# Another order of the pieces in a hand-listed attention and MLP kernel

## The chip, the core and the metric

The kernel runs on one core of a Trainium2 chip. The core has five engines that run their own instruction streams and wait for each other by semaphores: TensorE (PE in the profile; PEld is its weight load), VectorE (DVE), ScalarE (ACT), GpSimd (POOL) and SyncE (SP), which here only issues DMAs. The metric is the device time of one execution in microseconds. Three timed runs of the kernel before gave 219.97, 220.22 and 221.33 us; the median is 220.22.

## The reference

The input x has 2048 rows (tokens) of 512 bfloat16 values. The result is x + A(n) + B(n), where n is x after a layer norm without weights.

```
xn = layernorm(x)                                # rows of 512
A: q, k, v = xn @ wq, xn @ wk, xn @ wv           # 32 heads of 16
   for each of 4 segments of 512 tokens:
     p     = softmax(q k^T / 4 + mask)           # mask: 0 on and below the diagonal, -1e9 above
     a_dot = p v
     a_mem = (phi(q) M) / (phi(q) z + 1e-6)      # phi(t) = t + 1 if t > 0 else exp(t)
     o     = g a_mem + (1 - g) a_dot             # g = sigmoid(beta), one per head
     M, z += phi(k)^T v, sum of phi(k)
   A = o @ wo
B: silu(xn @ w1) @ w2                            # 1792 hidden columns
out = x + A + B
```

## The kernel before

The whole program is a list of some 1350 words, `ORDER`, that is walked once. Each word names a piece, a Python function that issues the few instructions of one step, with its indices: `h0.3.1` is part 1 of hidden tile 3 of segment 0. The word order is the program order of every engine at once: it fixes the order in which each engine runs its own instructions, the order of the DMAs on SP's queue, and the order in which the buffers of each pool are taken (the buffer that was given back first, in the order of the list, is taken first). The engines then run as far ahead of each other as their semaphores let them.

The pieces, with the lines that matter:

- `S0` to `S71` (`scores`): one batch of attention logits, 18 a segment in two groups of nine. TensorE multiplies q and k in four row groups (L724) into `psS`, a tile of four PSUM banks of which there is only one; ScalarE takes the exponential of all 2048 columns (L730, `Pb`); GpSimd zeroes what is above the diagonal (L744). The next batch can be multiplied only when this exponential has been read out of `psS`.
- `k`, `q`, `v`, `h` (`dense`, `dense_mm`): parts of the projections and of the hidden layer, by L336 (whole array) or L338 (four column strips of 32). A part of `k`, `q`, `v`, `h` in segments 0 and 1 is one product's worth of 512 columns, in segments 2 and 3 two. The result of a group of parts stands in one of the four PSUM banks of the pool `pp` until it is taken out.
- Taken out by VectorE: `kv`, `qv`, `vv` (copies, L376, L399, L406), `hv` (L497, with the tanh of `ha`, L492 on ScalarE, before it), `Ev`, `Ov` (L821, L828); by ScalarE: `ka`, `qa`, `va`, `Ea`.
- `E`, `O` (`weigh`, L791): weights times values for even and odd heads; `Om` (L835) merges the odd heads on VectorE.
- `fp`, `fa`, `fv` and `gp`, `ga`, `gv`: phi of k and of q on GpSimd, ScalarE and VectorE (L433); `t` turns phi(k) by a DMA; `m`, `mv`, `mw`: the memory M; `s`, `sv`, `r`, `w`, `R`, `W`, `z`, `zv`, `d`, `dv`, `n`, `nv`: denominators, their spreading by DMAs, and the sums with the memory's part (`zv` L589, `dv` L599, `nv` L608, `R` L560, `W` L566).
- `xs`, `xg`, `Nv`, `XD`: statistics (L286, L289), root (GpSimd) and normalisation (L315) of a tile of 128 tokens, and its transposition by a DMA (L857) for tiles 4 to 15. The first four tiles are transposed on TensorE (`X`, L845).
- `o`, `oc`, `od`, `oh`: full, half and quarter products of the two output projections; `st`, `sh` add x and store. `xl` loads x again. `lw0`, `lw1` load w2 and wo from ScalarE's queue (L169).

Whether a dense product is issued whole or in four strips follows from the words around it (`ahead`, `now`): products next to `E`, `O`, `s` and `m` are issued in strips.

Of the kernel before, what the change touches and what calls it, by code (L numbers as in the profile page):

```python
# [25 lines left out]
S6 fa0.3 k1.2.0 k1.2.1 k1.2.2 h0.5.0 h0.5.1 h0.5.2 q1.1.0 h0.5.3 ha0.5 k1.2.3 kv1.2 q1.1.1 q1.1.2 hv0.5
S8 h0.7.0 q1.1.3 qv1.1 h0.6.0 h0.6.1 h0.6.2 h0.6.3 ha0.6 fv0.3 E1 Ev1 k1.0.0
S9 hv0.6 h0.7.1 h0.7.2 h0.7.3 Om0 ha0.7 k1.0.1 k1.0.2 kp1.2 q1.0.0 q1.0.1 q1.0.2 fp0.1 Nv9 XD9 xs12 k1.0.3 kv1.0 kp1.0
S10 h0.8.0 hv0.7 h0.8.1 h0.8.2 h0.8.3 ha0.8 h0.9.0 h0.9.1 q1.0.3 t0.3 Nv10 XD10 h0.9.2 h0.9.3 qv1.0
S13 hv0.8 O1 Ov1 xs15 v1.0.0 v1.0.1 v1.0.2 ha0.9 v1.0.3 vv1.0 h0.10.0 h0.10.1 bmask  # L30
S12 k1.1.0 k1.1.1 k1.1.2 t0.2 k1.1.3 kv1.1 h0.10.2 h0.10.3 ha0.10 hv0.9 h1.0.0 Om1 h1.0.1 h1.0.2
# [16 lines left out]
S31 o0.0.4 h1.13.0 h1.13.1 h1.13.2 h1.13.3 ha1.13 o0.3.8 Om5 o0.3.11 o0.3.16 hv1.2 o0.3.9
S30 o0.3.14 h1.12.0 h1.12.1 h1.12.2 h1.12.3 t1.3 Nv15 hv1.13 ha1.12 XD15 od0.0.0.0 o0.1.16 od0.1.8.2 o0.1.17 o0.1.12 hv1.12 oc0.1.9.0
S33 o0.0.1 od0.1.8.3 o0.3.1 xl0.1 od0.1.8.0 st0.0 oc0.1.3.0 o0.1.13 oc0.1.3.1 xl0.3 gp1.3 Om4 fa1.0 o0.1.2 E6 o0.1.0  # L50
S32 kp2.3 Ev6 O6 Ov6 o0.3.17 o0.3.13 o0.3.10 o0.1.6 oc0.3.2.1 o0.1.15 m1.2 fa2.0 mv1.2 fv1.0
S35 o0.1.4 q2.2.0 q2.2.1 qv2.2 fp2.0 ga1.3 v2.0.0 v2.0.1
S34 h1.5.0 h1.5.1 o0.1.14 o0.1.11 t1.0 vv2.0 h1.5.2 oc0.3.0.1 xl1.0 gv1.3 fp1.1 h1.5.3 ha1.5 E7
# [889 lines left out]
```

## Time and profile before

| | |
|---|---|
| timed runs, us | 219.97, 220.22, 221.33 (median 220.22) |
| profiled execution, from its first to its last instruction | 218.2 us |
| median less that span | 2.0 us |
| TensorE busy | 210.9 us, 97% of the span, 3982 matmuls recorded |
| weight loads busy | 116.1 us, 4006 instructions |
| VectorE busy | 181.3 us, 83% |
| ScalarE busy | 184.1 us, 84%; of this the 72 exponentials 135.2 us |
| GpSimd busy | 127.4 us, 58% |
| DMA queues | 19.60 MB, 33273 packets |

Columns of the profile's groups: line, engine, operation, output and inputs, shapes, count, then busy time, mean ns of one, and the idle time of the engine ahead of them with what ended it. In a timeline the columns are start, length, engine, line and operation with the count merged into the row. A busy TensorE is not TensorE at its peak: matmuls are pipelined and their recorded ends overlap the next ones.

### The profile page before, as it was taken

The numbers are of one execution on the slowest core, as the hardware profiler recorded it, in microseconds if no ns is written. First come the engines' busy times: TensorE is split into PE (matmuls) and PEld (weight loads), VectorE is DVE, ScalarE is ACT, GpSimd is POOL, SyncE is SP. The second block draws the span as 40 slices with busy tenths as digits, with TensorE's granted clock in tenths as the row PEclk, the third lists the DMA queues.
The fourth block names the chain that finished last, engine by engine and source line by source line (L and its number), as shares of the span: only waits on it lengthen the run. The fifth ranks groups of instructions, "written<-read, shape, count | busy, mean of one in ns | idle before, by whom it ended". The sixth has DMA issues, their size and how long they took to land.

```text
span 218.2 us, 9267 instructions
## 1 busy us (share of the span) xinstructions
PE 210.9 (97%) x3982; PEld 116.1 (53%) x4006; DVE 181.3 (83%) x370; ACT 184.1 (84%) x173; POOL 127.4 (58%) x203
## 2 busy tenths in 40 slices
PE   7899999999999999999999999999999999999994
PEld 7666656655544544455444545445464544465653
DVE  6899999999799899667979886887979897858844
ACT  3799999999999999999999999999989998942000
POOL 6067676789568984697766436962787473410000
PEclk9999999999999999999999999999999999999999
DMA  6996249322200430541125131420042120412223
GB/s 183 344 375 160 51 125 243 74 53 53 51 5 17 157 71 10 117 95 40 49 67 83 54 97 28 74 77 6 0 132 73 52 73 13 131 32 79 84 66 98
DMA packets 33273, 19.60 MB, mean 90 GB/s; under 512 B 14672, under 2 KB 33232, under 8 KB 33232
## 3 DMA queue, kind: packets, MB, share of 16 engines
q1 hardware_dynamic: 30608, 16.39, 28.7%
q10 hardware_dynamic: 2624, 2.62, 3.8%
...
q14 instruction: 10, 0.08, 0.1%
HBM read 9.96 MB, written 2.10 MB: 55 GB/s over the span
## 4 chain that ended last, share of the span: by engine, by line
PE 92%; DMA 3%; ACT 2%; issue 1%; SPq 1%; DVE 0%
PE ps L336 26%; PE psO L338 17%; PE ps L338 16%; PE psS L724 11%; PE psO L336 9%; PE psV L791 8%; PE psS L338 4%; DMA wk_sb<-in_A_wk_dram 3%; ACT Pb L730 2%; PE psM L452 1%; SPq L169 0%; SPq L158 0%; PE ps L509 0%; ACT th L492 0%; DVE o_half L668 0%
## 5 line engine op out<-in xcount | busy, mean ns | idle before, releaser
L730 ACT ACTIVATE Pb<-psS 128x2048 bf16<-128x2048 f32 x72 | 135.2, 1878 | 4.7 <-PE psS L724 2.4
L744 POOL TENSOR_SCALAR_AFFINE_SELECT Pb<-Pb 128x512 bf16<-128x512 bf16 (+2 forms) x88 | 62.3, 718 | 22.4 <-ACT Pb L730 19.6
L497 DVE SCALAR_TENSOR_TENSOR hT<-th,ps 128x512 bf16<-128x512 bf16 x56 | 38.0, 682 | 10.1 <-ACT th L492 9.4
L744 POOL TENSOR_SCALAR_AFFINE_SELECT lows<-Pb 64x512 bf16<-64x512 bf16 (+1 forms) x40 | 24.3, 607 | 32.0 <-ACT Pb L730 24.9
L338 PE MATMUL psO<-w_sb,hT 128*32 128x512 bf16 (+2 forms) x696 | 41.4, 321 | 0.0
L336 PE MATMUL ps<-xnT,w_sb 128*128 128x512 bf16 (+1 forms) x177 | 35.9, 330 | 0.2 <-issue 0.2
L492 ACT ACTIVATE th<-ps 128x512 bf16<-128x512 f32 x56 | 33.0, 594 | 3.5 <-PE ps L338 3.1
L338 PEld LDWEIGHTS <-hT 128*32 128x32 bf16 x864 | 21.5, 96 | 14.6 <-issue 3.1
L338 PE MATMUL ps<-xnT,w_sb 128*32 128x512 bf16 (+1 forms) x408 | 24.8, 349 | 0.0
L724 PE MATMUL psS<-qT,k 32*128 32x64 bf16 (+3 forms) x512 | 23.0, 233 | 0.2
L336 PEld LDWEIGHTS <-w_sb 128*128 128x128 bf16 x178 | 16.4, 98 | 11.9 <-issue 1.2
L336 PE MATMUL psO<-w_sb,hT 128*128 128x512 bf16 (+2 forms) x82 | 20.5, 324 | 0.7 <-issue 0.6
L791 PEld LDWEIGHTS <-Vz 128*32 128x32 bf16 x768 | 16.1, 97 | 9.5 <-issue 0.6
L791 PE MATMUL psV<-Pb,Vz 128*32 128x448 bf16 (+7 forms) x512 | 21.0, 286 | 0.0
L724 PEld LDWEIGHTS <-k 32*128 32x128 bf16 x512 | 9.3, 92 | 21.2 <-issue 20.4
L336 PE MATMUL ps<-xnT,wk_sb 128*128 128x256 bf16 (+1 forms) x63 | 14.4, 326 | 0.4 <-DMA wk_sb<-in_A_wk_dram 0.2
L724 PE MATMUL psS<-qT,kT 16*128 16x448 bf16 (+3 forms) x256 | 14.7, 269 | 0.0
L338 PEld LDWEIGHTS <-w_sb 128*32 128x32 bf16 x408 | 10.3, 96 | 6.7 <-issue 1.7
L621 DVE SCALAR_TENSOR_TENSOR o_out<-psO,x_res 128x512 bf16<-128x512 f32 x14 | 9.4, 679 | 5.0 <-PE psO L338 3.9
L336 PEld LDWEIGHTS <-hT 128*128 128x128 bf16 x92 | 8.5, 98 | 9.6 <-issue 2.1
L828 DVE CAST odd<-psV 128x512 bf16<-128x512 f32 x16 | 11.0, 687 | 2.4 <-PE psV L791 2.4
L338 PE MATMUL psO<-wo_sb,oT 128*32 128x512 bf16 x140 | 12.8, 379 | 0.0
...
## 6 DMA issues: line engine op xcount, KB each, us to landing
...
```

Source lines behind the costliest of these rows:

```text
L336: return [nc.tensor.matmul(out, lhsT=lhsT, rhs=rhs, start=start, stop=stop, skip_group_check=True)]
L338: nc.tensor.matmul(out[c : c + 32], lhsT=lhsT[:, c : c + 32], rhs=rhs, start=start, stop=stop, tile_position=(0, c), skip_group_check=True,)
L452: nc.tensor.matmul(psM[32 * g : 32 * g + 32, i, :].rearrange("p (r d) -> p r d", d=DH), lhsT=st["phiK", dt][:, j, 32 * g : 32 * g + 32], r ...
L492: nc.scalar.activation(out=th[:], in_=sts[s]["h", ft][:, :], func=AF.Tanh, scale=0.5)
L497: nc.vector.scalar_tensor_tensor(out=st["hT"][:, ft, :], in0=st.pop(("th", ft))[:], scalar=1.0, in1=st.pop(("h", ft))[:, :], op0=ALU.add, ...
L621: out = nc.vector.scalar_tensor_tensor(out=o_out[:], in0=st.pop(("psO", j)), scalar=0.5, in1=st["x", j][:], op0=ALU.mult, op1=ALU.add)
L724: nc.tensor.matmul(psS[:, g, c : c + q2 - q1], lhsT=keys[rows], rhs=st["qT"][rows, dt, q1:q2], start=True, stop=True, tile_position=(32 * ...
L730: exp = nc.scalar.activation(out=blocks(Pb, b).rearrange("p y g c -> p g y c"), in_=psS[:, :, :].rearrange("p g (y c) -> p g y c", c=BLOCK ...
L744: over[id(Pb)].append(nc.gpsimd.affine_select(out=out, in_=in_, compare_op=ALU.is_ge, fill=0.0, base=base, pattern=[[0, out.shape[1]], [1, ...
L791: nc.tensor.matmul(psV[32 * g : 32 * g + 32, q0 : q0 + nq].rearrange("p (y c) -> p y c", y=weights.shape[2]), lhsT=Vzs[s % 2][:, kt, 4 * d ...
L828: copy(out=odd[:], in_=sts[s].pop(("psV", 1))[:, :])
```

## The change

Only the list is exchanged. The same 1349 words stand in it; each occurs once in both. Up to `v0.0.0` the two lists agree, and the order of `S0` to `S71` among themselves is the same in both. From there on nearly all other words may stand elsewhere. Some of the moves, cut from the list:

```diff
 ORDER = """
 ones0 ones1 zeros xc0 xd0 ... X1.1 Xa0.1 v0.0.0
-v0.0.1 v0.0.2 xs3 xi2 Nv2 xq3 xi3 v0.0.3 X2.1 Xa1.1 k0.1.0 tb Nv3 X3.1 Xv2.1 k0.1.1 Xv3.1 vv0.0 odd omask k0.0.0 ... xs5 ka0.1 kp0.1
-S0 v0.1.0 v0.1.1 xs6 xs7 q0.2.1 v0.2.1 v0.2.2 v0.2.3 vv0.2 fa0.0 k0.2.0 k0.2.1 k0.2.2 xs4 xg4.4
-S2 q0.2.2 q0.2.3 qv0.2 k0.2.3 kv0.2 fp0.2 fa0.2 v0.1.2 v0.1.3 vv0.1 Nv5 Nv6 XD6 q0.1.0 q0.1.1 q0.1.2 q0.1.3 qv0.1
-S1 h0.0.0 h0.0.1 h0.0.2 xs10 h0.0.3 v0.3.0 v0.3.1 v0.3.2 v0.3.3 ha0.0 vv0.3 q0.3.0 kp0.2 hv0.0
-S3 h0.3.0 h0.3.1 q0.3.1 q0.3.2 h0.3.2 tanh XD5 h0.3.3 k0.3.0 Nv7 XD7 q0.3.3 qv0.3 k0.3.1 xs8 ha0.3
-S4 Nv4 h0.1.0 k0.3.2 h0.1.1 hv0.3 XD4 h0.2.0 h0.2.1 h0.2.2 h0.2.3 ha0.2 xs9 k0.3.3 kv0.3 hv0.2
-S7 xs11 xg8.4 v1.2.0 v1.2.1 v1.2.2 v1.2.3 vv1.2 h0.1.2 h0.1.3 ha0.1 E0
...
-S17 h1.10.3 k1.3.0 hv1.0 k1.3.1 k1.3.2 k1.3.3 kv1.3 fp1.3 h0.12.0 h0.12.1 xs14 m0.2 mv0.2 ha1.10 h0.12.2
+xs3 xq3 xi2 v0.0.1 Nv2 Xa1.1 tb xi3 v0.0.2 Nv3 v0.0.3 X2.1 X3.1 k0.1.0 Xv2.1 k0.0.0 Xv3.1 ... vv0.0 q0.0.3 kf0.0 xs6 xs5 k0.1.2 xl0.0 ... xs4 v0.2.0 kp0.1
+S0 k0.2.0 xs7 v0.2.1 v0.2.2 k0.2.1 q0.2.1 v0.2.3 v0.1.0 fa0.0 v0.1.1 k0.2.2 xg4.4 vv0.2
+S2 q0.2.2 k0.2.3 v0.1.2 v0.1.3 q0.2.3 q0.1.0 q0.1.1 q0.1.2 kv0.2 q0.1.3 qv0.2 fa0.2
+S1 v0.3.0 h0.0.0 qv0.1 Nv4 v0.3.1 v0.3.2 XD4 vv0.1 h0.0.1 Nv6 h0.0.2 h0.0.3 v0.3.3 q0.3.0 fp0.2 Nv5 XD6 ha0.0 vv0.3 xs10 XD5
+S3 h0.3.0 h0.3.1 k0.3.0 h0.3.2 tanh h0.3.3 q0.3.1 ha0.3 k0.3.1 q0.3.2
+S4 k0.3.2 xs8 hv0.0 k0.3.3 q0.3.3 kp0.2 hv0.3 h0.2.0 h0.2.1 h0.2.2 h0.2.3 v1.2.0 kv0.3 ha0.2 lw0 Nv7 v1.2.1 qv0.3
+S7 h0.1.0 xs11 h0.1.1 hv0.2 v1.1.0 v1.2.2 h0.1.2 v1.2.3 vv1.2 h0.1.3 ha0.1 v1.1.1 xs9 xg8.4 E0 hv0.1 fv0.2
+S5 h0.4.0 XD7 h0.4.1 v1.1.2 v1.1.3 h0.4.2 q1.2.0 vv1.1 h0.4.3 Ev0 ha0.4 q1.2.1 q1.2.2 hv0.4
...
+S17 k1.3.0 k1.3.1 k1.3.2 xl0.2 k1.3.3 hv1.0 h1.10.3 ha1.10 XD10 Ov2 kv1.3 h0.12.0 h0.12.1 m0.2 kp1.1 kp1.3
...
```

In the list before, `lw0` stands in the stage of `S11`; in the new one in that of `S4`. `xl0.0`, which stood in that of `S14`, comes ahead of `S0`. `XD13` and `XD15` stood in the stages of `S27` and `S30` and now stand in those of `S35` and `S34`. Behind `S71` the order on VectorE was and is:

```diff
-hv3.13 R0.2 dv3.3 Ov15 R0.1 R0.3 st2.1 dv3.2 R0.0 W0 hv3.10 R1.0 hv3.6 dv3.1 zv3.2 R1.2 R1.3 nv3.2 R1.1 W1 zv3.1 nv3.1 zv3.0 Om15 nv3.0 zv3.3 nv3.3 st2.3 st3.0 st3.2 sh1 st3.1 sh0
+Om14 Om13 hv3.13 R0.3 R0.0 hv3.6 Ov15 R0.2 R0.1 W0 dv3.0 st2.1 dv3.2 R1.1 R1.3 hv3.10 zv3.2 R1.2 R1.0 dv3.1 Om15 W1 nv3.2 zv3.1 nv3.1 dv3.3 st2.3 zv3.0 nv3.0 zv3.3 nv3.3 st3.0 st3.2 sh1 st3.1 sh0
```

More of the change, by code (lines that the diff above doesn't have):

```diff
@@ L26 @@
[L26 to L31, printed above, removed]
@@ L48 @@
[L48 to L53, printed above, removed]
@@ new lines @@
+S11 q1.2.3 fp0.3 fv0.0 v1.3.0 v1.3.1 O0 k1.2.0 v1.3.2 fa0.1 Ov0 k1.2.1
+S6 k1.2.2 qv1.2 kind h0.5.0 h0.5.1 h0.5.2 k1.2.3 t0.2 gate h0.5.3 v1.3.3 q1.1.0 omask kv1.2 q1.1.1 ha0.5
+S8 h0.6.0 vv1.3 q1.1.2 h0.6.1 k1.0.0 q1.1.3 hv0.5 h0.6.2 kp0.3 qv1.1 h0.6.3 E1 Nv8 h0.7.0 fa0.3 Nv10 Ev1 ha0.6
+S9 h0.7.1 h0.7.2 h0.7.3 k1.0.1 k1.0.2 k1.0.3 q1.0.0 hv0.6 t0.0 ha0.7 q1.0.1 q1.0.2 fv0.3 kv1.0
+S10 xs15 h0.9.0 h0.9.1 h0.8.0 XD8 Nv9 h0.9.2 h0.8.1 h0.8.2 hv0.7 q1.0.3 XD9 h0.8.3 ha0.8 h0.9.3
+S13 v1.0.0 v1.0.1 kp1.0 t0.3 qv1.0 v1.0.2 bmask v1.0.3 hv0.8 O1 h0.10.0 h0.10.1 ha0.9
@@ new lines @@
+S12 vv1.0 xs12 k1.1.0 k1.1.1 k1.1.2 hv0.9 h0.10.2 Ov1 h0.10.3 h1.0.0 k1.1.3 h1.0.1 h1.0.2 ha0.10 kv1.1
+S15 E2 h1.10.0 h1.0.3 fp0.1 Nv11 h1.10.1 XD11 hv0.10 Ev2 h1.10.2 Om1 O2 ha1.0
+S17 k1.3.0 k1.3.1 k1.3.2 xl0.2 k1.3.3 hv1.0 h1.10.3 ha1.10 XD10 Ov2 kv1.3 h0.12.0 h0.12.1 m0.2 kp1.1 kp1.3
+S21 q1.3.0 q1.3.1 h0.12.2 xs14 q1.3.2 mv0.2 q1.3.3 h1.3.0 h1.3.1 h0.12.3 ha0.12 qv1.3 h1.3.2
+S14 gp1.2 h1.3.3 hv1.10 h0.13.0 ha1.3 hv0.12 xl0.3 xs13 k2.2.0 fv0.1 k2.2.1 h0.13.1 h0.11.0 h0.13.2
+S16 h0.11.1 h0.11.2 kv2.2 t0.1 hv1.3 fp1.3 Om0 kp1.2 h0.13.3 h0.11.3 q2.1.0 q2.1.1 qv2.1 E3 ha0.13 Ev3 ha0.11
```

108 lines of the change are left out of this document (54 added, 54 removed).

## The prediction

> **What bounds the kernel now.** I read the page first, its busy times and the chain, then the waits of TensorE, then timelines of single stages.
>
> ```profile
> span 218.2 us, 9267 instructions
> ...
> PE 210.9 (97%) x3982; PEld 116.1 (53%) x4006; DVE 181.3 (83%) x370; ACT 184.1 (84%) x173; POOL 127.4 (58%) x203
> ...
> PE 92%; DMA 3%; ACT 2%; issue 1%; SPq 1%; DVE 0%
> ```
>
> TensorE is busy for 97% of the span and is 92% of the chain that ended last. Idle are 218.2 - 210.9 = 7.3 us. The waits say where (first and last of six rows), and one row of the timeline shows the last matmul:
>
> ```profile
> PE psS L864 <- DVE zraw L188: 1.1, 1, 1.1
> ...
> PE ps L336 <- DVE z L468: 0.2, 1, 0.2
> ```
>
> ```profile
> 214.98 0.28 PE L338 MATMUL psS<-wo_sb,oT 128*32 128x256 bf16 x4
> ```
>
> 1.1 us lie ahead of the first matmul and 218.2 - 215.26 = 2.9 us behind the last, for the last evacuation and store; both ends are the same in the two lists. 3.3 us are left for the 214 us between. The only wait there for a piece of VectorE behind the start is 0.2 us. So the old order already feeds TensorE without a break, and a new order can win at most these 3.3 us. No word is added or removed: counted in the lists, both give the same products and 144 changes between whole-array, row-group and strip products, of the same four kinds; the new list issues six weight loads fewer.
>
> There is one more floor, which no wait shows. Here is the stage of `S4`, in which the old list has eight parts (`h0.1.0 k0.3.2 h0.1.1 h0.2.0 h0.2.1 h0.2.2 h0.2.3 k0.3.3`):
>
> ```profile
> 21.55 0.21 PE L724 MATMUL psS<-qT,k 32*128 32x64 bf16 x4
> 21.89 0.39 PE L336 MATMUL ps<-xnT,w_sb 128*128 128x256 bf16 x2
> 22.01 1.88 ACT L730 ACTIVATE Pb<-psS 128x2048 bf16<-128x2048 f32 x1
> 22.34 1.25 PE L336 MATMUL ps<-xnT,w_sb 128*128 128x256 bf16 x10
> 23.93 0.40 PE L724 MATMUL psS<-qT,k 32*128 32x64 bf16 x8
> ```
>
> `S7` starts at 23.93, 0.04 behind the end of the exponential at 22.01 + 1.88 = 23.89, since `psS` is a single tile. From `S4` to `S7` are 2.38 us: a stage can't be shorter, whatever stands in it. Ten matmuls of 256 columns take 1.25, of which the last alone is 0.38 at most, so one is (1.25 - 0.38)/9 = 0.10 to 0.11 and a part of two 0.216. The batch itself is 21.89 - 21.55 = 0.34, and with the change of mode behind the stage about 0.46. A stage of nine parts is 9 x 0.216 + 0.46 = 2.40, just above the floor; one of eight is 2.19 and wastes 0.19.
>
> **The change, part by part.**
>
> *Stages that are too short.* I filled each of the 71 stages of both lists with these prices (a quarter product 0.054, an `E` or `O` 0.54 for its 1280 columns in strips, an `m` 0.13) and added what is missing to 2.38. Old list: 0.19 in `S4`, 0.06 to 0.09 each in `S7`, `S13`, `S17`, `S24` and `S32`, some hundredths in three more: 0.7 us. New list: `S3` has eight parts (0.19), `S17` seven and an `m` (0.28, by 7 x 0.216 + 0.13 + 0.46 = 2.10), `S32` and `S61` 0.15 each, `S11`, `S13`, `S24` and `S43` 0.06 to 0.09 each: 1.1 us. A longer stage elsewhere doesn't pay it back, because TensorE takes the words in order. **Cost 0.4 us.** Below this it can go to 0, if the batch's own time is shorter there, and up to 0.6 by the rounding of eight stages.
>
> *The start.* The new list puts `X3.1` ahead of `k0.1.0`:
>
> ```profile
> 7.96 0.41 DVE L315 TENSOR_SCALAR xn_t<-x_lo,mv_all,rstd_all 128x512 bf16<-128x512 bf16 x1
> 8.54 0.39 PE L336 MATMUL ps<-xnT,wk_sb 128*128 128x256 bf16 x2 [0.24 <-DMA wk_sb<-in_A_wk_dram]
> 8.77 0.39 PE L845 MATMUL ptr<-ident,xn_t 128*128 128x128 bf16 x4
> ```
>
> TensorE waits 0.24 us for wk while tile 3 is normalised at 8.37. Moved ahead, the transposes start at about 8.45 and take the 0.22 us that they hold today (8.77 to the next product at 8.99), so `k0.1.0` starts at 8.67 and everything behind it 8.99 - 8.89 = 0.1 us earlier. **Gain 0.1 us**, between 0 and the 0.24 of the wait. The copies that follow on ScalarE move with it.
>
> *VectorE behind the start.* The list moves statistics and copies past each other, so what matters is whether a PSUM bank is free when the next product needs it.
>
> ```profile
> 11.51 0.69 DVE L286 BATCH_NORM_STATS2 stats<-x_hi 128x6 f32<-128x512 bf16 x1 [0.23 <-DMA x_hi<-in_A_x_dram]
> 12.34 0.66 DVE L286 BATCH_NORM_STATS2 stats<-x_hi 128x6 f32<-128x512 bf16 x1
> 15.32 0.69 DVE L399 CAST qT<-ps 128x512 bf16<-128x512 f32 x1
> 15.93 0.68 DVE L376 CAST kT<-ps 128x512 bf16<-128x512 f32 x1
> 16.88 0.66 POOL L744 TENSOR_SCALAR_AFFINE_SELECT Pb<-Pb 128x512 bf16<-128x512 bf16 x1
> 17.13 1.18 DVE L315 TENSOR_SCALAR xn_t<-x_hi,mv_all,rstd_all 128x512 bf16<-128x512 bf16 x2
> ```
>
> An `xs` costs 0.83, a copy that has another behind it 0.61, a norm 0.41 alone and 0.59 beside a GpSimd instruction. The new queue: four `xs` from 11.51 to 14.8; `vv0.2 kv0.2 qv0.2` to 16.65; `qv0.1` from 16.85, when its product is done (`S1` starts near 16.6); with `vv0.1`, `vv0.3` and three norms to 19.9 or 20.4. `k0.3.0` in the stage of `S3` needs the bank of `vv0.3` at 16.6 + 2.4 + 0.46 + 0.43 = 19.9. Then `xs10`, `xs8` to 21.6 or 22.1 and `hv0.0` to 22.2 or 22.8, whose bank `h0.2.0` wants at 21.4 + 0.46 + 0.65 = 22.5. So this is even or up to 0.5 late. That `xs9`, `xs11` and `xs12` stand later pays later, in a stretch without a wait. **I take 0.1 us**, between 0 and 0.5, as the two delays overlap and the norms stand beside little GpSimd work.
>
> *The transpositions and w2.* `XD4` to `XD7` go out later, and `lw0` five stages earlier.
>
> ```profile
> 18.33 6.26 SPq L857 DMA_TRANSPOSE xnT<-xn_t  x4
> 29.16 0.39 ACTq L169 DMA_DIRECT2D w_sb<-in_B_w_dram  x1
> ```
>
> ```profile
> 20.50:21.00 0.50, 0.50 (x7) 0.46 (x5) 0.50 (x2) 0.50 (x1) 0.50 (x1) 1.00 0.13 30
> ...
> 34.00:37.80 3.80, 3.75 (x88) 2.55 (x89) 3.70 (x8) 3.65 (x5) 2.22 (x4) 1.00 1.02 226
> ```
>
> The second fence is a table of stretches; its last two columns are the DMA engines' busy share and GB/s. The first transposition, issued at 18.33, has moved its data by about 20.5 (share 0.13 behind it): 2.2 us. In the new queue `Nv7` follows `hv0.0` by `hv0.3` and `kv0.3`, 22.2 + 1.2 + 0.4 = 23.8, so `XD7` has landed at about 26.0. Its first reader is `q1.2.0`, at 26.5 (`S5`: 21.4 + 2.4 + 2.7) + 0.46 + 5 x 0.216 = 28.0. **Cost 0**, with 2 us to spare; the price if w2 takes them is the first rival. w2 itself, `xl0.0`, `XD13` and `XD15` keep over 2 us.
>
> *The end.* In the old list `hv3.10` stands early. In the new one VectorE's last chain waits behind it: `h3.10.1` ends 13.3 us ahead of the last product (counted in columns), at 201.8 on the old clock.
>
> ```profile
> 203.06 0.55 DVE L560 RECIPROCAL ri<-zraw 32x64 f32<-32x64 bf16 x1
> 203.65 0.35 DVE L566 TENSOR_SCALAR rz<-ri,gate 32x256 bf16<-32x256 f32 x1
> 207.40 0.41 DVE L589 TENSOR_TENSOR oT<-spr,oraw 128x512 bf16<-128x512 bf16 x1
> 208.32 0.69 DVE L608 TENSOR_TENSOR oT<-ps,oT 128x512 bf16<-128x512 f32 x1 [0.50 <-PE ps L338]
> ```
>
> From there to `nv3.3`: a tanh 0.6, four `nv` and `hv3.10` and `st2.3` at 0.69, four `zv` and two `dv` at 0.41, two `R` at 0.55, `Om15` 0.45, `W1` 0.35: 9.1 us, less 0.08 for each overlapping pair, so `nv3.3` is done at about 210.0 to 211.5 (it may wait for `n3.0`, which is at 209.4). Its reader `o3.0.17` stands 3.2 us from the end, at 211.9; `o3.2.14`, at 210.6, reads what `nv3.0` writes some 1.0 earlier than `nv3.3`. Before, `nv3.3` ended at 209.0 and that reader stood at 209.7. **I take 0.1 us**, between 0 and 0.6.
>
> Sum: 0.4 - 0.1 + 0.1 + 0 + 0.1 = +0.5, so a span of 218.7. The median is 2.0 above the profiled span; with that kept, about **220.7 us**. What a measurement of this kernel can tell from no change is about 1%, 2.2 us.
>
> **The rivals.**
>
> *w2 delays the last transposition (slightly slower).* Today a transposition issued inside w2's load would have data only until 37.8, when the share of 1.02 ends: w2 is on the engines for over eight us behind its issue. In the new list `lw0` follows `ha0.2`, at about 24.3, half a us behind `XD7`. If `XD7` were stretched to 5 us it would land at 28.8 and `q1.2.0` would wait 0.8: 221.5 us. Against it, `XD7` is issued first and needs 2.2. [...]
>
> *VectorE slips at many banks (clearly slower).* How thin the old margins are shows one hand-over: the bank that `qv2.1` frees is taken by `h1.11.0`.
>
> ```profile
> 57.84 0.69 DVE L399 CAST qT<-ps 128x512 bf16<-128x512 f32 x1 [0.94 <-PE ps L338]
> ...
> 58.60 0.61 PE L338 MATMUL ps<-xnT,w_sb 128*32 128x512 bf16 x8
> ```
>
> It ends at 58.53 and TensorE starts at 58.60. In the new order other VectorE instructions meet GpSimd's. What this costs VectorE in all:
>
> ```profile
> L835 DVE COPY_PREDICATED oraw<-omask,odd 128x256 int32<-128x256 int32 x16 | 9.7, 606 | 0.0
> L589 DVE TENSOR_TENSOR oT<-spr,oraw 128x512 bf16<-128x512 bf16 x16 | 8.1, 510 | 0.9 <-DMA spr<-rz 0.9
> L315 DVE TENSOR_SCALAR xn_t<-x_hi,mv_all,rstd_all 128x512 bf16<-128x512 bf16 x8 | 4.1, 524 | 0.0
> ```
>
> ```profile
> 205.62 0.45 DVE L835 COPY_PREDICATED oraw<-omask,odd 128x256 int32<-128x256 int32 x1
> ```
>
> Against the undisturbed 0.45, 0.41 and 0.41 these lose 16 x 0.16 + 16 x 0.10 + 8 x 0.11 = 5.0 us, and none of it reaches TensorE today. If half falls in front of a full bank, +2.5: 223.2 us. It decides from the point where a delay exceeds the bank's margin of 0.1 to 0.5. For it speaks that a new order has new meetings; against it, that VectorE has slack on the whole (83%). [...]
>
> *The slips go (a little faster).* If the new order has none of the floors' extra cost and frees half of the 3.3 us: 220.2 - 1.6 + 0.5 = 219.1. Faster by over 1% needs 2.2 of 3.3 us.
>
> **How the numbers follow.** Forecast 0.60 (220.2 to 221.4); w2's delay 0.10 (221.5); many slips 0.17 (222.5 to 224); gains 0.13, of which 0.03 beyond 1%. The range from 219.1 to 223.2 leaves out half of the slips' case and some of the gains'. Faster 0.03, same 0.80, slower 0.17.
>
> **What would show it.** Right: no wait of TensorE over 0.3 us behind the start; `S4` and `S21` starting 0.05 behind an exponential's end; `k0.1.0` near 8.7; idle time of TensorE within 1 us of 7.3. Wrong: TensorE waiting for the transposition at about 28; a sum of waits for `kv`, `hv`, `Ov` and the like above 1.5 us; a late `nv3.0` or `nv3.3` in the last 5 us; a stage chain from `S0` to `S71` more than 1 us from today's plus 0.4.

## The result and the profile after

The changed kernel takes 228.8 us (median of 6 executions, 226.38 to 229.59) against 220.38 us (6 executions, 219.87 to 221.33): a ratio of 1.037, with a 95% interval of 1.0325 to 1.0409. The forecast was 220.7 us, with a range to 223.2. The profiled execution took 227.35 us, with a span of 225.6, 7.4 us above that of before.

First the page of the changed kernel: the span, TensorE's busy time and the chain that ended last by engine.

```profile
span 225.6 us, 9261 instructions
...
PE 213.4 (95%) x3975; PEld 117.1 (52%) x4000; DVE 180.5 (80%) x370; ACT 184.4 (82%) x173; POOL 125.0 (55%) x203
...
PE 79%; DVE 5%; issue 4%; DMA 4%; ACT 3%; POOL 3%; SPq 1%; DVEq 0%; POOLq 0%
```

TensorE's share of the chain falls from 92% to 79%; it idles 12.2 us instead of 7.3, and is busy 2.5 us longer with the same products. The waits of TensorE name the idle time (engine and line, releaser, us in total, times, longest); these are the first three rows.

```profile
PE ps L336 <- DMA xnT<-xn_t: 2.1, 1, 2.1
PE psO L336 <- DVE oT L589: 1.5, 1, 1.5
PE psS L864 <- DVE zraw L188: 1.1, 1, 1.1
```

Two waits are new: one for a transposition and one for a `zv`. The waits for VectorE's copies, of which one rival was made, stay at 0.3 us and below each. Where the 7.4 us lie follows from the first matmul of each batch, read off the timelines (us; the last column is the list of "All three together" below):

| stretch | before | after | three repairs |
|---|---|---|---|
| up to `S0` | 11.95 | 12.16 | 12.77 |
| `S0` to `S8` | 22.09 | 25.63 | 21.86 |
| `S8` to `S29` | 46.80 | 47.07 | 47.08 |
| `S29` to `S27`, one stage | 2.38 | 3.90 | 2.37 |
| `S27` to `S71` | 106.77 | 107.35 | 107.19 |
| `S71` to the end of the last matmul | 25.27 | 25.34 | 25.34 |
| behind the last matmul | 2.94 | 4.15 | 2.99 |
| span | 218.2 | 225.6 | 219.6 |

6.3 of the 7.4 us lie in three places: 3.5 between `S0` and `S8`, 1.5 in one stage, 1.2 behind the last matmul. The other 1.1 us are spread: 0.6 between `S27` and `S71`, 0.3 between `S8` and `S29`, 0.2 at the start.

**Ahead of S8.** The timeline of the changed kernel around `XD7`, and the chain's row for its transfer (start, length).

```profile
23.82 0.39 ACTq L169 DMA_DIRECT2D w_sb<-in_B_w_dram  x1
23.93 1.19 SPq L857 DMA_TRANSPOSE xnT<-xn_t  x1
...
30.55 0.52 PE L336 MATMUL ps<-xnT,wq_sb 128*128 128x512 bf16 x1 [2.10 <-DMA xnT<-xn_t]
```

```profile
23.93 6.58 DMA xnT<-xn_t
```

`lw0` goes out 0.11 us ahead of `XD7`. The transposition takes 6.58 us, where the three ahead of it took 2.5 to 2.9; it lands at 30.50, and `q1.2.0`, whose place is 28.45, waits 2.10 us. That is not all, as a table of stretches shows (busy time of each engine, then TensorE's granted clock, the DMA engines' share and GB/s):

```profile
29.00:30.00 1.00, 0.00 (x0) 0.00 (x0) 0.91 (x2) 0.19 (x1) 0.93 (x2) 1.00 1.15 361
...
31.00:32.00 1.00, 1.00 (x5) 0.31 (x3) 0.00 (x0) 0.47 (x1) 0.00 (x0) 0.50 0.49 151
...
33.00:34.00 1.00, 1.00 (x12) 0.31 (x8) 0.46 (x2) 1.00 (x1) 0.00 (x0) 0.50 0.06 16
34.00:35.00 1.00, 1.00 (x44) 0.64 (x40) 0.11 (x1) 1.00 (x2) 0.11 (x1) 0.95 0.00 0
```

Behind the wait TensorE's granted clock is 0.50 from about 30.7 to 34.1 us: 3.4 us at half speed, 1.7 us of work lost, and the greater part of the 2.5 us by which TensorE is busy longer. In the chain it hides in longer matmuls: a product of 256 columns (L336) took 417 ns in that stretch and 273 behind it.

**In the stage of S29.** The product that waits is `o0.2.14`, for `zv0.0`, which waits for the second DMA of `z0.0`:

```profile
85.98 0.52 DVE L589 TENSOR_TENSOR oT<-spr,oraw 128x512 bf16<-128x512 bf16 x1 [2.38 <-DMA spr<-rz]
...
86.78 0.38 PE L336 MATMUL psO<-wo_sb,oT 128*128 128x512 bf16 x1 [1.52 <-DVE oT L589]
```

SP's queue of the changed kernel, and then that of before (start, length of the whole run of issues, count):

```profile
74.59 2.68 SPq L577 DMA_DIRECT2D spr<-rz  x4
77.37 1.20 SPq L441 DMA_TRANSPOSE phiK<-pk  x1
78.67 1.16 SPq L813 DMA_DIRECT2D zraw<-oraw  x2
79.96 1.32 SPq L813 DMA_DIRECT2D zraw<-odd  x2
81.33 3.08 SPq L577 DMA_DIRECT2D spr<-rz  x4
```

```profile
70.78 3.94 SPq L577 DMA_DIRECT2D spr<-rz  x6
74.82 1.15 SPq L813 DMA_DIRECT2D zraw<-oraw  x2
76.02 1.34 SPq L577 DMA_DIRECT2D spr<-rz  x2
```

In both, the queue is nearly full from the first `spr<-rz` on. Before, `z0.0`'s DMAs are the ninth and tenth issue, behind one pair of sums; in the new list they are the twelfth and thirteenth, behind `t1.3` (the `phiK` row) and both pairs of sums, and the second goes out at 83.80.

**Behind the last matmul.** The last evacuations of the changed kernel, then of before:

```profile
220.96 0.69 DVE L621 SCALAR_TENSOR_TENSOR o_out<-psS,x_res 128x512 bf16<-128x512 f32 x1 [1.53 <-PE psS L338]
...
221.17 0.28 PE L338 MATMUL psS<-w_sb,hT 128*32 128x256 bf16 x4
221.57 0.42 DVE L668 SCALAR_TENSOR_TENSOR o_half<-psS,x_res 128x256 bf16<-128x256 f32 x1
221.90 0.68 DVE L621 SCALAR_TENSOR_TENSOR o_out<-psO,x_res 128x512 bf16<-128x512 f32 x1
...
222.50 0.42 DVE L668 SCALAR_TENSOR_TENSOR o_half<-psS,x_res 128x256 bf16<-128x256 f32 x1
```

```profile
213.24 0.69 DVE L621 SCALAR_TENSOR_TENSOR o_out<-psS,x_res 128x512 bf16<-128x512 f32 x1 [0.28 <-PE psS L338]
...
215.31 0.42 DVE L668 SCALAR_TENSOR_TENSOR o_half<-psS,x_res 128x256 bf16<-128x256 f32 x1 [0.18 <-PE psS L338]
```

Before, only `sh0` stands behind the last matmul. After, `st3.2` runs at 220.96, and `sh1`, `st3.1` and `sh0` queue on VectorE behind it, so that `sh0` starts 1.05 us behind the last matmul's end instead of 0.05. `st3.2`'s last product, `o3.2.17`, stands some 20 words ahead of the end.

### The profile page after: what moved, and what is told of

It reads as the page before. It is cut to its first block, busy times and chain, and to the rows that moved or that the text cites. A ratio compares the mean times of both kernels' runs of the same rounds, so it can differ in the third digit from the quotient of the medians.

```text
span 225.6 us, 9261 instructions
## 1 busy us (share of the span) xinstructions
PE 213.4 (95%) x3975; PEld 117.1 (52%) x4000; DVE 180.5 (80%) x370; ACT 184.4 (82%) x173; POOL 125.0 (55%) x203
## 3 DMA queue, kind: packets, MB, share of 16 engines
q10 hardware_dynamic: 2624, 2.62, 3.9%
## 4 chain that ended last, share of the span: by engine, by line
PE 79%; DVE 5%; issue 4%; DMA 4%; ACT 3%; POOL 3%; SPq 1%; DVEq 0%; POOLq 0%
PE ps L336 22%; PE psO L338 15%; PE ps L338 13%; PE psS L724 9%; PE psV L791 7%; PE psO L336 6%; PE psS L338 3%; DMA xnT<-xn_t 3%; PE psS L864 2%; ACT Pb L730 2%; POOL Pb L744 1%; DMA spr<-rz 1%; SPq L577 1%; ACT th L492 1%; POOL k L385 1%
## 5 line engine op out<-in xcount | busy, mean ns | idle before, releaser
L744 POOL TENSOR_SCALAR_AFFINE_SELECT Pb<-Pb 128x512 bf16<-128x512 bf16 (+2 forms) x88 | 61.2, 705 | 27.8 <-ACT Pb L730 25.0
L338 PE MATMUL psO<-w_sb,hT 128*32 128x512 bf16 (+2 forms) x692 | 44.3, 327 | 0.0
L744 POOL TENSOR_SCALAR_AFFINE_SELECT lows<-Pb 64x512 bf16<-64x512 bf16 (+1 forms) x40 | 23.1, 577 | 35.9 <-ACT Pb L730 32.2
L336 PE MATMUL ps<-xnT,w_sb 128*128 128x512 bf16 (+1 forms) x173 | 37.8, 333 | 0.7 <-issue 0.6
L338 PE MATMUL ps<-xnT,w_sb 128*32 128x512 bf16 (+1 forms) x416 | 26.0, 345 | 0.0
L336 PEld LDWEIGHTS <-w_sb 128*128 128x128 bf16 x176 | 16.3, 98 | 12.6 <-issue 2.0
L336 PE MATMUL psO<-w_sb,hT 128*128 128x512 bf16 (+2 forms) x86 | 21.2, 313 | 0.5 <-issue 0.5
L336 PE MATMUL ps<-xnT,wq_sb 128*128 128x256 bf16 (+1 forms) x58 | 13.5, 332 | 2.3 <-DMA xnT<-xn_t 2.1
L336 PE MATMUL ps<-xnT,wk_sb 128*128 128x256 bf16 (+1 forms) x62 | 14.0, 325 | 0.3 <-issue 0.2
L336 PEld LDWEIGHTS <-hT 128*128 128x128 bf16 x93 | 8.7, 98 | 9.8 <-issue 1.5
```

The lines of the kernel that those rows point to most:

```text
L336: return [nc.tensor.matmul(out, lhsT=lhsT, rhs=rhs, start=start, stop=stop, skip_group_check=True)]
L338: nc.tensor.matmul(out[c : c + 32], lhsT=lhsT[:, c : c + 32], rhs=rhs, start=start, stop=stop, tile_position=(0, c), skip_group_check=True,)
L744: over[id(Pb)].append(nc.gpsimd.affine_select(out=out, in_=in_, compare_op=ALU.is_ge, fill=0.0, base=base, pattern=[[0, out.shape[1]], [1, ...
```

## The experiments

Times are medians; the kernel before had 220.54 us on the chip that ran w2 late, w2 early, `z` early and the end, 220.54 on that of `XD7` early, `z` late, the three together and their five filled stages, and 220.39 on that of the other four.

### w2 late in the new list, and early in the old one

```diff
-S4 ... kv0.3 ha0.2 lw0 Nv7 v1.2.1 qv0.3
+S4 ... kv0.3 ha0.2 Nv7 v1.2.1 qv0.3
-S11 ... v1.3.1 O0 k1.2.0 ...
+S11 ... v1.3.1 O0 lw0 k1.2.0 ...
```

> The new list with one word moved back: lw0 (w2's load) stands behind O0 in the stage of S11 instead of behind ha0.2 in that of S4. Theory A (w2's packets share the DMA engines with XD7 and make it 6.6 us long): XD7, issued near 23.9, lands near 26.4 as the undisturbed ones do (2.4 to 2.9 us); TensorE's wait of 2.1 us for it goes, and with it the stretch of 3.5 us at half the granted clock; S0 to S8 takes 22.1 us instead of 25.6, the span falls by about 3.5 us from 225.6, and the median by about 4.5 (2.1 of wait, and a mean of 2.4 lost to the clock, from the granted clocks of 0.985 to 0.998 of the six executions): near 224.3. The spread of the executions falls below 1 us. Rival B (XD7 is late by itself, because it is issued 23.9 us in, behind other work, whatever w2 does): its landing stays near 30 and the time near 228.8. Rival C (w2 now comes too late for the products that read it): a new wait at the first o words in the stage of S18.

Measured: 224.2 us (223.96 to 225.46), ratio 1.0178 (1.0147 to 1.0209). `XD7`, issued at 23.66, landed at 26.11. `S0` to `S8` took 21.88. The first row of TensorE's waits, and two stretches:

```profile
PE psO L336 <- DVE oT L589: 2.3, 1, 2.3
```

```profile
28.00:30.00 2.00, 2.00 (x31) 0.89 (x33) 2.00 (x5) 1.98 (x3) 1.86 (x3) 1.00 0.00 0
...
32.00:34.00 2.00, 2.00 (x20) 1.13 (x19) 1.90 (x10) 2.00 (x2) 0.80 (x3) 1.00 1.05 366
```

The wait and the slow stretch are gone, TensorE is busy throughout. Theory A holds in its numbers. `XD7` is not late by itself (rival B), and no product waited for w2 (rival C). The transposition that now meets the load, `phiK` issued at 32.80, took 6.1 us, and no product waits for it there.

```diff
-S4 Nv4 h0.1.0 ... h0.2.3 ha0.2 xs9 k0.3.3 kv0.3 hv0.2
+S4 Nv4 h0.1.0 ... h0.2.3 ha0.2 lw0 xs9 k0.3.3 kv0.3 hv0.2
-S11 ... XD8 O0 lw0 kp0.3 ...
+S11 ... XD8 O0 kp0.3 ...
```

> The opposite: the list before with the same word moved from the stage of S11 to behind ha0.2 in that of S4, nothing else. Theory A: the last transposition of tiles 4 to 7 (XD4, issued at 23.3, landed at 25.7) meets w2's load and lands near 29.5; its first reader q1.2.0 stands at about 29.2, so TensorE waits 0 to 0.5 us only, and the time is 220.4 to 221.2: w2's early load by itself costs little, and costs what it does in the new list because q1.2.0 also stands a stage earlier there. XD8, which took 5.5 us inside w2's load, then takes about 2.5. Rival B (w2 doesn't stretch a transposition): XD4 lands at 25.7 as before.

Measured: 221.33 us, ratio 1.0041 (1.0022 to 1.006).

```profile
23.71 1.59 SPq L857 DMA_TRANSPOSE xnT<-xn_t  x1
24.02 0.39 ACTq L169 DMA_DIRECT2D w_sb<-in_B_w_dram  x1
```

```profile
30.69 0.83 PE L338 MATMUL ps<-xnT,wq_sb 128*32 128x512 bf16 x12 [1.21 <-DVE hT L497]
```

`XD4`, issued 0.3 us ahead of w2, landed at 30.64, after 6.9 us, and TensorE's first `q1.2` product starts at 30.69. The row names `hv0.4`, which ended at 30.65; in the list before the same product ran ahead of that word's end (29.03 against 30.22), so it doesn't need it, and the landing is what released it. `XD8`, out of the load's way, took 2.4 us instead of 5.5. So w2's load stretches a transposition in either list. It cost 1.2 us of wait here and 2.1 in the new list, where `q1.2.0` stands a stage earlier; the wait was larger than I expected (0 to 0.5), because the transfer was.

### The transposition out of w2's way

```diff
-S3 h0.3.0 h0.3.1 k0.3.0 h0.3.2 tanh h0.3.3 ...
+S3 h0.3.0 h0.3.1 k0.3.0 h0.3.2 tanh Nv7 XD7 h0.3.3 ...
-S4 ... ha0.2 lw0 Nv7 v1.2.1 qv0.3
+S4 ... ha0.2 lw0 v1.2.1 qv0.3
-S5 h0.4.0 XD7 h0.4.1 ...
+S5 h0.4.0 h0.4.1 ...
```

> The new list with w2's load left where it is, early, and the transposition XD7 taken out of its way: Nv7 and XD7 stand behind tanh in the stage of S3, some 2 us ahead of lw0. Theory A (only transpositions that are on the DMA engines together with w2 are stretched): XD7 is issued near 22, lands near 24.5 (2.5 to 2.9 us), q1.2.0 doesn't wait; S0 to S8 22.1 us; the wait on zv0.0 (1.5 to 2.3 us) and the end stay, so about 224.3, as with w2 late. Rival B (the early w2 costs by other ways too, such as x tiles or sums that share the engines): more than 225.5, with another DMA named in the waits between 24 and 33.

Measured: 226.19 us, ratio 1.0256 (1.0223 to 1.0288). `XD7` was issued at 22.61, 1.8 us ahead of w2 (24.41), and landed at 26.83, after 4.2 us; `q1.2.0` didn't wait. `XD5` ahead of it took 4.7, and `v1.1.0` waited 0.36 for it; since `XD5` also took 4.5 us in an execution with w2 late, this run doesn't say how much of either delay is w2's. Against w2 late, the profiled span is 1.9 us longer: 0.8 up to `S0`, 0.5 between `S0` and `S71`, and 0.6 behind `S71`, with a wait of 0.4 for an `nv`; and two of its four executions had a granted clock of 0.992. Theory A is right on the wait for `XD7` and 1.9 us short in the time. By its two signs, a time over 225.5 and another DMA among the waits, rival B came; but the wait that it names is 0.36 us, and the start's 0.8 is none of the edit's, since nothing ahead of `S0` differs. Whether the early w2 costs more than the wait for `XD7` stays open.

### The rows of z on SP's queue

```diff
-S20 ... z0.3 ... z0.2 E4 ha1.1
-S28 ... O4 Ov4 z0.1 kp2.2 o0.0.8
-S26 ... Nv12 z0.0 ...
+S20 ... z0.3 ... z0.2 z0.1 z0.0 E4 ha1.1
+S28 ... O4 Ov4 kp2.2 o0.0.8
+S26 ... Nv12 ...
```

> The new list with z0.1 and z0.0 (from the stages of S28 and S26) moved directly behind z0.2 in that of S20, ahead of t1.3 and of the sums of E4 and O4 on SP's queue. Theory A (zv0.0 is late because z0.0's two DMAs stand behind nine other issues on SP's queue): z0.0 is issued near 78.5 instead of 83.1, zv0.0 runs where its word stands, TensorE's wait of 1.5 us ahead of o0.2.14 goes, S29 to S27 takes 2.4 us instead of 3.9, and the time falls by 1.5 to about 227.3 (the spread of the clock, 3 us, lies over it, so the stage is read and not the median alone). Rival B (the wait moves to what is pushed back: t1.3, or E4's and O4's sums): 228.8, with another wait of 1 us or more in the stages up to S31.

Measured: 224.41 us, ratio 1.0197 (1.0148 to 1.0245). SP's queue:

```profile
73.27 5.26 SPq L577 DMA_DIRECT2D spr<-rz  x8
78.62 1.20 SPq L441 DMA_TRANSPOSE phiK<-pk  x1
```

`S29` to `S27` took 2.38 us, and no other wait took its place. So theory A is right on the wait. The median fell by 4.4 us, though, three times the wait. In this list `XD7`'s wait was 1.7 us and no slow stretch followed it in the profiled execution; the section on the clock accounts for most of the rest.

```diff
-S28 ... mw0.2 t1.3 oc0.2.5.1 Ev4 ...
+S28 ... mw0.2 oc0.2.5.1 Ev4 ...
-S30 ... h1.12.3 oc0.3.0.0 ...
+S30 ... h1.12.3 t1.3 oc0.3.0.0 ...
```

> The new list with one word moved: t1.3, the transposition of phi(k) that stands ahead of E4's and O4's sums and of z0.1 and z0.0 on SP's queue, goes back behind h1.12.3 in the stage of S30, where the list before has it too. In e3_z_early all ten... issues that stood ahead of z0.1 were passed at once; this takes away one of them, 1.2 to 2.2 us long in the traces so far. Theory A (t1.3 is the greater part): z0.0's two DMAs go out 1.2 to 2.2 us earlier and the wait on zv0.0 falls from 1.5 to 2.3 us to 0 to 0.4; the list before with both z words behind O4's sums but without t1.3 ahead of them waited only 0.25. Rival B (the sums of E4 and O4 make it late, since they wait for E4 and O4 themselves): over 1 us of wait stays. The time itself is blurred by the clock behind XD7's wait: 224.4 to 227 by A.

Measured: 225.05 us, ratio 1.0206 (1.0177 to 1.0234).

```profile
74.47 2.68 SPq L577 DMA_DIRECT2D spr<-rz  x4
77.24 1.14 SPq L813 DMA_DIRECT2D zraw<-oraw  x2
78.48 1.07 SPq L813 DMA_DIRECT2D zraw<-odd  x2
79.59 2.63 SPq L577 DMA_DIRECT2D spr<-rz  x4
```

The issues of `z0.1` and `z0.0` begin 5.1 us behind the first `spr<-rz` instead of 6.7, `zv0.0` waits 0.44 us and TensorE not at all: `S29` to `S27` is 2.38. The one word `t1.3` is the difference between a wait of 1.5 to 2.3 us and none.

The opposite, in the list before:

```diff
-S20 ... gv1.1 kp2.0 z0.1
-S28 ... Ev4 Om3 z0.0 ... O4 Ov4
+S20 ... gv1.1 kp2.0
+S28 ... Ev4 Om3 ... O4 Ov4 z0.1 z0.0
```

> The opposite of e3_z_early, in the list before: z0.1 and z0.0 moved behind Ov4 in the stage of S28, so that their four issues stand behind the sums of E4 and O4 on SP's queue, as in the new list. Theory A (the place on SP's queue makes zv0.0 late): z0.0 lands some 2 us later than in the list before, o0.2.14 or the product ahead of it waits 1 to 2 us, the time is 1 to 2 us above before, 221.5 to 222.5. Rival B (in this list there is room for it): within 0.3 of before.

Measured: 220.63 us, ratio 1.0006 (0.9986 to 1.0027): rival B. Without `t1.3` ahead of them the late `z` words cost 0.25 us in the stage of `S29` and nothing that the times can tell in all. So it is not the place behind E4's and O4's sums that hurts; these use up the room, and `t1.3` goes beyond it.

### The end

```diff
-... o3.2.17 oh5.0 oh5.1 oh17.1 o3.1.5 o3.1.17 oh11.1 o3.1.13 o3.1.14 oh16.0 oh13.0 oh1.0 oh2.0 st3.2 oh14.0 sh1 oh15.0 oh10.0 oh17.0 oh12.0 st3.1 sh0
+... o3.2.17 st3.2 oh5.0 oh5.1 oh17.1 o3.1.5 o3.1.17 oh11.1 sh1 o3.1.13 o3.1.14 st3.1 oh16.0 oh13.0 oh1.0 oh2.0 oh14.0 oh15.0 oh10.0 oh17.0 oh12.0 sh0
```

> The new list with the last three evacuations moved ahead: st3.2 directly behind o3.2.17, sh1 behind oh11.1, st3.1 behind o3.1.14, each directly behind its last product. Theory A (the evacuation waits for whatever TensorE wrote into psS ahead of its word, so that four of them pile up behind the last product): from the end of the last matmul to the end of the span 3.0 us instead of 4.15, time lower by 1.1, about 227.7. Rival B (what is late behind the last matmul is the last store's own DMA): 4.1 us stays, 228.8.

Measured: 226.93 us, ratio 1.0277 (1.0232 to 1.0322).

```profile
221.91 0.28 PE L338 MATMUL psS<-w_sb,hT 128*32 128x256 bf16 x4
...
222.25 0.42 DVE L668 SCALAR_TENSOR_TENSOR o_half<-psS,x_res 128x256 bf16<-128x256 f32 x1 [0.29 <-PE psS L338]
222.70 0.33 SPq L672 DMA_DIRECT2D out_dram<-o_half  x1
```

From the last matmul's end (222.19) to the end of the span (225.2) are 3.0 us instead of 4.15. Theory A: an evacuation waits for what was written into `psS` ahead of its word, not for its own last product. The median fell by 1.9 us, 0.7 more than the place explains; with the clock taken off, as the section on it does, it is 1.0.

### All three together

The edits of w2 late, `z` early and the end early, in one list.

> The new list with the three repairs together: lw0 behind O0 in the stage of S11, z0.1 and z0.0 behind z0.2 in that of S20, and the three last evacuations directly behind their last products. Theory A (these three places are the whole of the loss beyond the forecast): no wait of TensorE over 0.4 us behind the start, granted clock 1.000 in every execution while TensorE works, 3.0 us behind the last matmul, S0 to S71 178.8 us (181.1 of the list with w2 alone moved, less 2.3 for zv0.0) against 178.0 before; time 224.2 - 2.3 - 1.1 = 220.8, that is +0.3 against before, between 0 and +1.0. Rival B (many small slips of VectorE, spread over the list, are a part of the loss): 222 to 223.

Measured: 221.25 us (12 executions, 220.46 to 222.05), ratio 1.0027 (1.001 to 1.0043). All waits of TensorE:

```profile
PE psS L864 <- DVE zraw L188: 1.1, 1, 1.1
PE ps L336 <- DMA wk_sb<-in_A_wk_dram: 0.4, 1, 0.4
PE ps L338 <- DVE oraw L821: 0.3, 1, 0.3
PE ps L336 <- ACT xnT L851: 0.2, 1, 0.2
```

That is theory A; the time that rival B gave, 222 to 223, didn't come. Three moves of six words take back 7.5 of 8.4 us. Of what is left, 0.7 us against the kernel before on the same chip, `S0` to `S71` at 178.50 us against 178.04 is 0.46. The remaining 0.25 isn't located: `S0` came 0.8 later in this execution than in that of before, but over the executions of the new list it varies by as much.

### What is left: stages under the floor

On top of the three repairs:

```diff
-S4 k0.3.2 xs8 hv0.0 ...
+k0.3.2 S4 xs8 hv0.0 ...
-S7 h0.1.0 xs11 ...
+h0.1.0 S7 xs11 ...
-S21 q1.3.0 q1.3.1 ...
+q1.3.0 S21 q1.3.1 ...
-S14 gp1.2 h1.3.3 hv1.10 ...
+h1.3.3 S14 gp1.2 hv1.10 ...
-S16 h0.11.1 h0.11.2 ...
+h0.11.1 S16 h0.11.2 ...
```

> As e5_all3, with five batches moved by one part each so that the two shortest stages are filled: S4, S7, S21, S14 and S16 each stand one word later (behind k0.3.2, h0.1.0, q1.3.0, h1.3.3 and h0.11.1). This tests the term of 0.4 us for stages below the floor of 2.38 us, of which S3 (0.19) and S17 (0.28) are the half. Theory A: S7 to S5 takes 0.2 us less than in e5_all3 (2.72 there by the traces so far), S16 to S19 0.2 to 0.3 less than 2.72, S0 to S24 0.4 to 0.5 us less in all, and the time is 0.4 below e5_all3. Rival B (the floor costs nothing because the batch's own time is shorter there): the same time within 0.15.

Measured: 221.35 us, ratio 1.0032 (1.0015 to 1.0049): no gain, which by the time alone is rival B. The stages say more. `S3` to `S4` took 2.40 with nine parts against 2.38 with eight, and `S16` to `S19` fell from 2.72 to 2.50; but `S17` with one part more grew by 0.33, so it had not been short, and the weights of `v1.1.0` waited 0.7 us for `XD5`, which landed at 25.93. Two further runs separate these. The first only moves `v1.1.0`, on top of the three repairs:

```diff
-S7 h0.1.0 xs11 h0.1.1 hv0.2 v1.1.0 v1.2.2 h0.1.2 v1.2.3 vv1.2 h0.1.3 ...
+S7 h0.1.0 xs11 h0.1.1 hv0.2 v1.2.2 h0.1.2 v1.2.3 vv1.2 v1.1.0 h0.1.3 ...
```

> As e5_all3, with v1.1.0 moved behind v1.2.3 and vv1.2 in the stage of S7. v1.1 is the first reader of XD5, whose landing varied from 23.7 to 26.0 us (2.9 to 4.7 us behind its issue) while v1.1.0 stands near 25.1; in the executions with the late landing S7 to S5 took 3.1 instead of 2.7 us. Theory A (an execution in two or three loses 0.4 us there): S7 to S5 at or below 2.72 in the trace, and the median 0.1 to 0.3 below e5_all3's, 221.0 to 221.2. Rival B: no change within 0.1.

Measured: 221.16 us (220.85 to 221.73), ratio 1.0028 (1.0011 to 1.0045): within 0.1 of the three repairs alone, rival B. The second adds the fill of the stage of `S3`:

```diff
-S4 k0.3.2 xs8 hv0.0 ...
+k0.3.2 S4 xs8 hv0.0 ...
-S7 h0.1.0 xs11 ...
+h0.1.0 S7 xs11 ...
```

> As e10_all3_v, with S4 one word later (behind k0.3.2) and S7 one word later (behind h0.1.0): the stage of S3, the shortest, then has nine parts and that of S7 one less. In e7_all3_filled S3 took 2.40 with nine parts against 2.38 with eight, but S7 took 3.1 through XD5's late landing, and S17 was longer by 0.33 with a ninth part, so it wasn't short. Theory A (the floor of S3 wastes 0.2): S7 to S5 falls to 2.50 and S0 to S11 by 0.2 us against e10_all3_v; the time by 0.2. Rival B: S0 to S11 the same within 0.05, because S7's end is set by something other than its number of parts.

Measured: 220.63 us (220.37 to 221.67), ratio 1.0012 (0.9997 to 1.0026). The first matmuls of `S7` and `S5`, without the fill and with it:

```profile
24.15 0.40 PE L724 MATMUL psS<-qT,k 32*128 32x64 bf16 x8
...
26.88 0.21 PE L724 MATMUL psS<-qT,k 32*128 32x64 bf16 x4
```

```profile
24.35 0.40 PE L724 MATMUL psS<-qT,k 32*128 32x64 bf16 x8
...
26.85 0.21 PE L724 MATMUL psS<-qT,k 32*128 32x64 bf16 x4
```

2.73 against 2.50, and `S0` to `S11` 17.09 against 16.89: the part that fills the short stage is free, and the stage it comes from is 0.2 shorter. The median falls by 0.5, more than the 0.2 of the trace; where the rest went isn't shown. The trace can't show it: the profiled execution was the slowest of this list (221.67), with a wait of 0.7 us for an `hv` at 78.7 that the trace without the fill doesn't have. This list can no longer be told from the kernel before.

The same on the list before, whose short stage is that of `S4`:

```diff
-S7 xs11 xg8.4 v1.2.0 v1.2.1 ...
+v1.2.0 S7 xs11 xg8.4 v1.2.1 ...
-S5 h0.4.0 h0.4.1 ...
+h0.4.0 S5 h0.4.1 ...
-S11 hv0.4 q1.2.0 q1.2.1 ...
+q1.2.0 S11 hv0.4 q1.2.1 ...
-S6 fa0.3 k1.2.0 k1.2.1 ...
+k1.2.0 S6 fa0.3 k1.2.1 ...
```

> The list before with its own short stage filled: S7, S5, S11 and S6 one word later each (behind v1.2.0, h0.4.0, q1.2.0 and k1.2.0), so that the stage of S4 has nine parts instead of eight, and that of S6, which takes 2.83 us, one less. Theory A (a stage of eight parts wastes 0.19): S4 to S7 stays at 2.38 to 2.41, S6 to S8 falls to 2.6, S0 to S8 is 0.2 below the 22.1 of before, and the time 0.2 below before, about 220.35: a small gain that five rounds can hardly tell. Rival B: S0 to S8 unchanged.

Measured: 220.44 us, ratio 0.9999 (0.9982 to 1.0015): rival B. `S6` to `S8` fell from 2.83 to 2.62, but `S4` to `S7` rose from 2.39 to 2.65. The ninth part is not free there: the next batch came 0.26 us later. `v1.2.0` is a product of another kind than its neighbours; that this is why is not shown.

No list beat the kernel before.

## The clock

Each execution has its mean granted clock. The table sets it beside TensorE's waits for `XD7` and for `zv0.0` in the profiled execution, whose clock stands first in its row:

| list | wait for `XD7`, us | wait for `zv0.0`, us | granted clock of its executions |
|---|---|---|---|
| new | 2.1 | 1.5 | 0.992, 0.985, 0.988, 0.998, 0.991, 0.985 |
| end early | 1.9 | 2.3 | 0.992, 0.992, 1.000, 0.992 |
| `XD7` early | none | 2.1 | 0.998, 0.992, 0.992, 1.000 |
| `t1.3` late | 2.1 | none | 0.989, 1.000, 0.996, 1.000 |
| `z` early | 1.7 | none | 0.996, 1.000, 0.989, 0.997 |
| w2 late | none | 2.3 | 1.000, 0.999, 1.000, 1.000 |
| three repairs | none | none | twelve from 0.998 to 1.000 |

A mean of 0.992 is 0.008 x 225.6 = 1.8 us lost, one stretch of 3.4 to 3.6 us at half speed; 0.985 is 3.4, by the same arithmetic two of them. Taking (1 - clock) x span off the six spans of the new list leaves 223.8 to 224.9 us, against 224.7 to 227.9 as measured: most of this kernel's spread is the clock. (The mean also counts a fall behind the last matmul, which costs nothing: in the trace of `z` early, with its 0.996, the clock is 0.50 only from 220.6 us on, 2.2 behind the last matmul. The 0.998 of `XD7` early is 0.4 us lost, too little for such a stretch.)

So a wait of some 2 us was followed by 3.4 us at half speed in some executions and not in others, and then cost 1.7 us more. The traces show what set these cases apart. In the trace of the new list the stretches at one clock last 23.89, 3.41 and 191.15 us, which is 7, 1 and 56 times 3.413; in that of before one lasts 215.04, to 1.7 us behind the span's end, 63 times; the slow stretches of the end early (87.20 to 90.61) and of `t1.3` late (31.40 to 34.81) are 3.41 long as well. One such step of 3.413 us, counted from the changes of the clock in a trace, is called a window below. Its place differs: a window begins at 4.87 us in the trace of before and at 6.79 in that of the new list. The length of the wait alone doesn't tell the cases apart; the idle time in one window does. Here are two neighbouring windows of the new list, with the wait for `XD7` whole in the first, and two of w2 late, where the wait of 2.3 us for `zv0.0` lies across the edge at 82.98. The columns are those of the table of stretches above, TensorE's busy time first.

```profile
27.27:30.68 3.41, 1.26 (x8) 0.73 (x10) 2.60 (x7) 1.88 (x1) 3.10 (x5) 1.00 1.12 343
30.68:34.09 3.41, 3.41 (x29) 1.04 (x31) 1.30 (x3) 1.75 (x2) 0.09 (x1) 0.50 0.27 82
```

```profile
79.57:82.98 3.41, 1.66 (x44) 0.72 (x32) 0.28 (x2) 3.38 (x3) 2.00 (x5) 1.00 0.39 101
82.98:86.39 3.41, 2.85 (x32) 1.24 (x37) 3.35 (x8) 1.13 (x3) 1.85 (x4) 1.00 0.04 7
```

For the eight waits of the table above, this is TensorE's idle time in the window that holds the most of each, and the clock in the next window:

| list, wait | its length, us | window | idle in it, us | next clock |
|---|---|---|---|---|
| end early, `zv0.0` | 2.3 | 83.79 to 87.20 | 2.16 | 0.50 |
| new, `XD7` | 2.1 | 27.27 to 30.68 | 2.15 | 0.50 |
| `t1.3` late, `XD7` | 2.1 | 27.99 to 31.40 | 2.13 | 0.50 |
| w2 late, `zv0.0` | 2.3 | 79.57 to 82.98 | 1.75 | 1.00 |
| new, `zv0.0` | 1.5 | 85.29 to 88.71 | 1.49 | 1.00 |
| end early, `XD7` | 1.9 | 29.18 to 32.59 | 1.26 | 1.00 |
| `z` early, `XD7` | 1.7 | 29.47 to 32.89 | 1.24 | 1.00 |
| `XD7` early, `zv0.0` | 2.1 | 80.30 to 83.71 | 1.09 | 1.00 |

The windows at the ends of the traces fit too: that of `z` early from 217.21 to 220.62, idle for 2.17 us behind the last matmul, is followed by 0.50, and that of before from 213.09 to 216.50, idle for 1.24, by 1.00. Of the windows named here those with 2.13 us idle or more were followed by half the clock and those with 1.75 or less were not; none lies between, and whether it is the idle time itself that counts isn't told. The window at half speed in the new list (30.68 to 34.09), in which TensorE was busy throughout, was followed by the full clock. What sets the place of the windows isn't shown; it differs between the traces, and one list has executions with a slow stretch and without. Of the executions without a trace only the mean clock is known.

The mean of the six clocks, 0.990, is 2.3 us lost in the new list's usual execution. The clock also explains why the single repairs add up to more than the three together: 4.6 + 4.4 + 1.9 = 10.9 against 7.55. Either of the first two takes away one wait and most of the clock's loss with it. With the clock's loss taken off, the median spans fall by about 2.0, 2.2 and 1.0, in all 5.1, against 4.9 for the three.

## Why the prediction was wrong

- **The bound.** TensorE bounds the kernel, and the list could win 3.3 us at most: nothing here contradicts it, and since no list gained, nothing tests it. The rest of the old order's trace was a sound base: with three places mended, the new list is 0.7 us above before, where the sum had said 0.5.
- **Stages that are too short, +0.4.** The size came out, but partly by luck: `S0` to `S71` is 0.46 longer in the repaired list, and only 0.2 of it, in the stage of `S3`, is shown to come from a short stage. The list of stages was partly wrong. `S17`, put down as 0.28 short, was not: one part more made it 0.33 longer, so its `m` must cost more than the 0.13 I gave it, by changes of kind around it or otherwise; and in the old list the ninth part of `S4` is not free.
- **The start, -0.1.** Not seen. `k0.1.0` started at 8.87, not near 8.7, and `S0` came at 12.16. Over the runs of the new list `S0` varies from 11.9 to 12.8 with the landing of x and wk, which is more than the term.
- **VectorE behind the start, +0.1.** No bank made TensorE wait there, and the rival of many slips found nothing. The 0.1 itself is too small to be seen in these runs.
- **The transpositions and w2, 0.** This is the step that failed, and it was the first rival, with a chance of 0.10; the wait, from 28.45 on, is also the first of its signs of being wrong. Put at nothing, it cost 2.1 us of wait and 1.7 of clock in the trace. `XD7`'s issue (23.8 forecast, 23.93 measured) and the place of `q1.2.0` (28.0 and 28.45) were right. The landing was not: 30.50 instead of 26.0. I had put against the rival that `XD7` is issued half a us first and needs only 2.2 us. It was issued 0.11 us behind w2, and with w2 late it took 2.45, so the 2.2 read off the DMA engines' share was a little short too; and in the old list with w2 early, a lead of 0.3 us didn't keep `XD4` from taking 6.9. The old trace had held the answer in `XD8`, 5.5 us inside w2's load; I used it for the rival's price, as 5 us, and not for the forecast. In the traces a transposition issued inside w2's load or up to 0.3 us ahead of it took 5.5 to 6.9 us; the others of before and of the new list took 2.4 to 4.5, most of them under 3. The two runs with w2 moved show that its load lengthens them; by what way is not shown. The price of the rival was too small for a second reason: nothing in the old trace showed the half clock, which is 1.00 there to the end of the span.
- **The end, +0.1.** The chain that I followed, `nv3.0` and `nv3.3`, made no product wait in the trace after (0.4 us in one other execution of that end). What I left out is the place of `st3.2`, `sh1` and `st3.1` among the last products: 1.15 us. I quoted the evacuations' floor of 2.9 us as "the same in the two lists", and that sentence is wrong.
- **What was not in the sum at all.** `z0.1`, `z0.0` and `t1.3` on SP's queue: 1.5 to 2.3 us. I had checked the moves of VectorE's words and of the big DMAs, but not counted the queue of small ones, which is full for 10 us (74.59 to 84.41).
- **The range.** It ended at 223.2, the worst of single rivals. Three independent misses and the clock together gave 228.8; the range had no case in which two of them come at once, and none in which a wait costs more than its length.
